# Linear attention, routed experts and a cosine layer in one program: values two slots behind the key maxima, a different pace of columns, routing in PSUM, four output buffers, rounding on DVE

## The chip, the cores and the metric

One Trainium2 chip, one of its cores. The metric is the device time of one execution in microseconds (us), as the median of several runs of the same program. All inputs start in device memory, and the result must lie there at the end. A core has TensorE (PE in the rows; PEld is its weight load), VectorE (DVE), ScalarE (ACT), GpSimd (POOL) and SyncE (SP, which here only issues transfers). Each engine takes its instructions strictly in the order in which they stand in its queue.

## The reference

Three layers follow one another. Attention without a score matrix (8 batches, 8 heads, 576 positions, 64 dimensions):

```
q_s = exp(q - max(q, -1));  q_s /= sum(q_s, -1) + 1e-9
k_s = exp(k - max(k, 2));   k_s /= sum(k_s, 2) + 1e-9
kv = einsum('bhsd,bhse->bhde', k_s, v)
x  = einsum('bhsd,bhde->bhse', q_s, kv)
```

Then 8 experts with two chosen per token (4608 tokens of width 512, inner width 1024), where the choice uses noisy logits:

```
noisy = x @ w_gate + log1p(exp(x @ w_noise)) * noise
top2 of noisy, softmax over the two -> weights
out += weight * (max(x @ w1[e], 0) @ w2[e])
```

And a last layer over all tokens with inner width 2048: `h = x @ w_in`, `y = (h * cos(h)) @ w_out`.

`w_in` and `w_out` come as 64-bit floats and are rounded to 32 bits on the chip.

## The kernel before

**Attention.** The keys of a batch are worked in two halves of four heads, so there are 16 half batches, and a loop gives each of them a slot `s`. `k_stage` takes one half batch: ACT copies half of the keys into PSUM (`kc`), DVE folds the four position groups and the 64 tail rows (`ktl`) into maxima `km` (L271 to L274), PE transposes `km` (`pkm`), DVE reduces it (`m`), PE spreads the maxima back over the partitions (`pkb`), ACT copies them (`mb`), POOL subtracts them from the keys, and ACT takes the exponential. `kv_stage` multiplies keys by values into `pkv` (L313), and after the second half of a batch DVE divides by the sums into `kvn` (L319 to L321). `kg_stage` transposes `kvn` on PE (`pkt`, L329) and multiplies it by the gate and noise weights (`pkg`), so that a token's logits come out with its x. The queries of 128 tokens form a column, and there are 36. `x_unit` transposes the queries of a column (`pqt`, ACT makes `qtt` of it), multiplies them by `kvn` into `px`, which has a single buffer, and DVE makes x (`xs`) and the logits (`lg`) of it (L392 to L398). The table `COLS` says how many columns each slot takes: 18 in the loop, 18 after it.

**Routing.** `routing` runs in three parts, after columns 18, 27 and 36. It is a chain of small DVE instructions on tiles of 144 or 72 elements per partition with a few ACT functions and matmuls between them, and ends in lists of tokens per expert. The first list lets the first three groups of tokens of expert 0 start while columns are still worked.

**Experts.** A group is up to 512 tokens of one expert. Per 128 inner elements a step does 12 matmuls into `ph` (`mm1`), ACT takes `hh` = relu, DVE takes the remainder `hl`, and two steps later 3 matmuls per 128 tokens go into `acc` (`mm2`). Numbers are kept as a pair of 32-bit values of reduced precision, high and low, hence three products. At a group's end `acc` is copied to a staging tile `ys`, by ACT for even blocks and by DVE for odd ones, and SP stores it to `y_d`. The next group's tokens are gathered by POOL into `xg`, moved by SP in four transfers per block (`xl<-xg`) and transposed by DVE. `w_load` brings expert weights through `wst` tiles; ACT makes the high part, POOL the low part. `convert` rounds the 64-bit weights in 64 pieces in the background of the first experts: SP loads `c`, ACT takes the magnitude (`ca`, L813), DVE does seven instructions, and SP stores the result from `cw`.

**Order.** The code is written in the order of the slots and steps, but a scheduler decides the final place of each instruction in its engine's queue, so a moved line can shift its neighbours too.

Of the kernel before, what the change touches and what calls it, by code (L numbers as in the profile page):

```python
# [10 lines left out]
F32 = mybir.dt.float32  # L11
# [16 lines left out]
def tile_attention_moe_moe2(  # L28
# [96 lines left out]
    def w_load(e):  # L125

        pend = []
        w1h, w1l, w2h, w2l = W[e % 2]

        def split():  # L130
            (kind, i, fh, _), st = pend.pop(0)
            if kind == 0:
                hi, lo = w1h[:, i, fh * 512:(fh + 1) * 512], w1l[:, i, fh * 512:(fh + 1) * 512]
            else:
                hi, lo = w2h[:, i, :], w2l[:, i, :]
            nc.scalar.activation(hi, st, AF.Copy)  # L136
# [40 lines left out]

    KB = 5
    QEB = 4
# [81 lines left out]
    def k_stage(j):  # L261
# [148 lines left out]
    def routing(t):  # L410
# [25 lines left out]
        nc.scalar.activation(ln, t1, AF.Ln)  # L436

        tiny = 2.0 ** -25
        d = tmp("rd")
# [5 lines left out]
        nc.vector.scalar_tensor_tensor(ln, z, 0.0, ln, op0=ALU.max, op1=ALU.add)  # L445
        yield
        tt(ln, ln, nzc, ALU.mult)
        l = tmp("ra")
        tt(l, ln, g, ALU.add)

# [3 lines left out]
        m2 = tmp("rm2", [P, n, 2, E])  # L454
        ta = tmp("rt1")
        for s in range(2):
# [26 lines left out]
        w2 = W2[:, cs, :]  # L483
        nc.vector.tensor_scalar(w2[:, :, 0], ex, 1.0, EPS, op0=ALU.add, op1=ALU.add)
        nc.vector.reciprocal(w2[:, :, 0], w2[:, :, 0])
        tt(w2[:, :, 1], ex, w2[:, :, 0], ALU.mult)
        yield
# [193 lines left out]

    HT = {}
    after = []

# [78 lines left out]
    def mm2(g, f):  # L763
# [42 lines left out]
    def convert():  # L806
        pend = []
        V = nc.vector

        def magnitude():  # L810
            t = pend[-1][1]
            ab = late[1].tile([P, CW], F32, name="ca", bufs=2)
            nc.scalar.activation(ab, t.bitcast(F32).rearrange("p (n w) -> p n w", w=2)[:, :, 1], AF.Abs)  # L813
            return ab

        def half1(ab):
# [12 lines left out]
        def half2(lo, bits, ab):  # L829
            dst = pend.pop(0)[2]  # L830
            w = late[1].tile([P, CW], F32, name="cw", bufs=2)
            V.tensor_single_scalar(ab, bits, -2 ** 23, op=ALU.bitwise_and)
            V.scalar_tensor_tensor(w, lo, 2.0 ** -52, ab.bitcast(F32), op0=ALU.mult, op1=ALU.mult)
            V.tensor_tensor(w, w, bits.bitcast(F32), op=ALU.add)
# [8 lines left out]
        for src, dst in jobs:  # L843
# [3 lines left out]
            if len(pend) == 2:  # L847
                yield
                z = half1(ab)
                ab = magnitude()  # L850
                yield
                half2(*z)
            else:
                ab = magnitude()
        yield
        half2(*half1(ab))

    C2 = 2.0 * math.pi - C1
    MAGIC = 1.5 * 2.0 ** 23
    magic = consts.tile([P, 1], F32, name="magic")  # L860
    nmagic = consts.tile([P, 1], F32, name="nmagic")
# [91 lines left out]
    presets(True)  # L953
    load_kv(1)
    load_kv(2)
    load_half(0, "q")
    load_kv(3)
    load_half(1, "q")
    load_kv(4)
    load_half(2, "q")  # L960
    COLS = {3: 1, 4: 2, 5: 2, 6: 2, 7: 1, 8: 2, 9: 1, 10: 2, 11: 1, 12: 1, 13: 1, 14: 1, 15: 1}
    QLOAD = {0: (3,), 2: (4, 5), 4: (6, 7), 11: (8,), 12: (9,), 13: (10,)}
    QST = {2: (0, 1), 4: (2, 3), 7: (4, 5), 9: (6, 7), 14: (8,), 15: (9,)}
    n = 0
    for s in range(2 * B + 1):
        if s < 2 * B:
            ks = k_stage(s)
            next(ks)
        if s >= 1:
            kv_stage(s - 1)  # L970
        if s == 0:
            load_small()
        if s >= 2 and s % 2 == 0:
            kg = kg_stage(s // 2 - 1)
            next(kg)
        if s in (4, 8):
            load_tail(s // 4 + 1, "k")
            load_tail(s // 4 + 1, "v")
        if s + KB < 2 * B:
            load_kv(s + KB)  # L980
        if s in (2, 6, 14):
            load_tail((2, 6, 14).index(s), "q")
        if s < 2 * B:
            finish(ks)
        if s >= 2 and s % 2 == 0:
            finish(kg)
        if s == 0:
            presets(False)
        next(cg, None)
# [4 lines left out]
        if s in (6, 11):  # L994
            q_tail((6, 11).index(s))
        for _ in range(COLS.get(s, 0)):
            x_unit(n)
            n += 1
    kp.release()
# [5 lines left out]
    mo = tc.alloc_tile_pool(name="mo", bufs=1, reuse_waits="tile")  # L1005
    for lst, name, k_, dt in ((HH, "hh", LAG + 1, F32R), (HL, "hl", LAG + 1, F32R), (YS, "ys", 2, F32)):
        lst += [mo.tile([P, 512], dt, name=f"{name}{j}") for j in range(k_)]
# [151 lines left out]
```

## Time and profile before

| | |
|---|---|
| median of 3 runs | 1955.85 us (1952.77 to 1956.34) |
| the profiled execution | 1950.03 us |
| its span, first to last instruction | 1947.9 us |
| busy: PE, DVE, ACT, POOL | 1822.6, 1135.4, 878.5, 450.6 us |
| mean granted TensorE clock | 0.958 |

The span is the profiled part of the execution; 2.1 us lie around it. The profiled execution was 5.8 us below the median of the runs. PE is busy for 94% of the span, so what can be gained lies where it waits, or where its clock is granted at 0.5 (1.2 GHz) and not at 1.0 (2.4 GHz). A busy sum over the whole span hides that the stages have different limits, so the stages are read apart.

### The profile page before, as it was taken

To read this page: it belongs to the slowest core of one execution; us is meant where nothing else is said; L and a number is where in the kernel's file an instruction comes from. 1 tells how busy PE (TensorE), PEld (TensorE's weight loads), DVE (VectorE), ACT (ScalarE), POOL (GpSimd) and SP (SyncE) were. 2 spreads that over 40 slices of the span, in tenths; PEclk is the share of its full clock that TensorE was granted. 3 is DMA by queue.
4 is the path that set the end of the run, shared out by engine and by line. 5 is a ranking of instruction groups with operands and counts; after the bars stand their busy time and mean duration, and the time that the engine had idled before them with its cause. 6 is when DMAs were issued, how large, how long until landed. Compare 5 with 4: busy or idle time off the path is not lost. (4 is left out here: it accounts for less than half of the span.)

```text
span 1947.9 us, 27149 instructions
## 1 busy us (share of the span) xinstructions
PE 1822.6 (94%) x9738; PEld 1535.1 (79%) x9738; DVE 1135.4 (58%) x2079; ACT 878.5 (45%) x1569; POOL 450.6 (23%) x405
## 2 busy tenths in 40 slices
PE   5777898989899999999999989999999999999998
PEld 4665787777777788989888878888888888888886
DVE  5768767776767743423333346665656565665654
ACT  4443333323224233232414256666666666666654
POOL 5445433504114023140405142110101010110000
PEclk7767899999999999999999999999999999999999
DMA  9942336645544434242425342202112030201000
GB/s 283 301 129 77 128 114 211 200 142 183 164 137 157 150 105 134 86 141 82 135 85 155 97 126 69 82 23 64 45 42 66 22 87 7 80 28 49 1 22 23
DMA packets 179776, 206.20 MB, mean 106 GB/s; under 512 B 34224, under 2 KB 121264, under 8 KB 179632
## 3 DMA queue, kind: packets, MB, share of 16 engines
q1 hardware_dynamic: 166896, 163.44, 27.1%
q0 software_dynamic: 12160, 39.86, 7.1%
q8 instruction: 82, 1.34, 0.3%
q10 hardware_dynamic: 576, 1.05, 0.1%
q14 instruction: 62, 0.51, 0.1%
HBM read 127.06 MB, written 49.43 MB: 91 GB/s over the span
## 5 line engine op out<-in xcount | busy, mean ns | idle before, releaser
L747 PE MATMUL ph<-xh,w1h 128*128 128x512 f32 (+2 forms) x1376 | 491.6, 357 | 7.4 <-DVE r L693 5.7
L748 PE MATMUL ph<-xl,w1h 128*128 128x512 f32 (+2 forms) x1376 | 491.3, 357 | 5.3 <-DVE xl L679 5.2
L749 PE MATMUL ph<-xh,w1l 128*128 128x512 f32 (+2 forms) x1376 | 491.2, 357 | 0.0
L771 PE MATMUL acc<-w2h,hh 128*128 128x512 f32 x1152 | 457.7, 397 | 23.6 <-ACT hh L753 8.7
L772 PE MATMUL acc<-w2l,hh 128*128 128x512 f32 x1152 | 453.5, 394 | 0.0
L773 PE MATMUL acc<-w2h,hl 128*128 128x512 f32 x1152 | 428.1, 395 | 13.6 <-DVE hl L754 13.0
L747 PEld LDWEIGHTS ph<-xh,w1h 128*128 128x128 f32 x1376 | 261.3, 190 | 47.5 <-DVE r L693 6.5
L748 PEld LDWEIGHTS ph<-xl,w1h 128*128 128x128 f32 x1376 | 261.5, 190 | 44.4 <-DVE xl L679 5.7
L749 PEld LDWEIGHTS ph<-xh,w1l 128*128 128x128 f32 x1376 | 261.8, 190 | 32.0
L771 PEld LDWEIGHTS acc<-w2h,hh 128*128 128x128 f32 x1152 | 218.6, 190 | 73.2 <-ACT hh L753 14.3
L773 PEld LDWEIGHTS acc<-w2h,hl 128*128 128x128 f32 x1152 | 216.7, 189 | 68.2 <-DVE hl L754 22.2
L754 DVE SCALAR_TENSOR_TENSOR hl<-ph,hh 128x256 fp32r<-128x256 f32 (+2 forms) x200 | 107.1, 539 | 259.5 <-ACT hh L753 259.2
L772 PEld LDWEIGHTS acc<-w2l,hh 128*128 128x128 f32 x1152 | 218.9, 190 | 40.0
L693 DVE SCALAR_TENSOR_TENSOR r<-r,ph 128x512 f32<-128x512 f32 x144 | 99.0, 687 | 142.6 <-ACT r L692 141.9
L616 POOL DMA_INDIRECT xg<-x_d,idx x80 | 78.1, 976 | 446.4 <-DVE xl L679 338.8
L753 ACT ACTIVATE hh<-ph 128x256 fp32r<-128x256 f32 (+2 forms) x200 | 93.0, 470 | 190.1 <-PE ph L749 185.2
L691 ACT ACTIVATE r<-r 128x512 f32<-128x512 f32 x144 | 90.7, 630 | 148.6 <-DVE r L690 148.6
L760 DVE TENSOR_TENSOR hl<-r,hh 128x512 fp32r<-128x512 f32 x144 | 99.3, 689 | 87.9 <-ACT hh L759 87.8
L616 POOL DMA_INDIRECT xg<-y_d,SL x36 | 34.8, 968 | 425.2 <-DVE xl L679 390.8
L137 POOL TENSOR_TENSOR w1l<-wst,w1h 128x512 fp32r<-128x512 f32 x80 | 103.1, 1312 | 123.0 <-ACT w1h L136 120.9
L689 DVE SCALAR_TENSOR_TENSOR r<-kk,ph 128x512 f32<-128x512 f32 x144 | 98.7, 685 | 48.9 <-ACT kk L688 48.6
L678 ACT ACTIVATE xh<-xg 128x512 fp32r<-128x512 f32 x106 | 66.6, 628 | 124.6 <-DVE xg L675 124.2
(184 smaller groups left out, 2208.5 us busy)
## 6 DMA issues: line engine op xcount, KB each, us to landing
wst<-in_moe_w_dram SPq DMA_DIRECT2D x128, 256.0 KB, 3.2
xl<-xg SPq DMA_DIRECT2D x396, 64.0 KB, 2.2
y_d<-ys SPq DMA_DIRECT2D x72, 256.0 KB, 2.3
kt<-in_k_dram SPq DMA_DIRECT2D x16, 512.0 KB, 6.7
vt<-in_v_dram SPq DMA_DIRECT2D x16, 512.0 KB, 7.2
qt<-in_q_dram SPq DMA_DIRECT2D x16, 512.0 KB, 7.2
x_d<-xs SPq DMA_DIRECT2D x32, 256.0 KB, 2.8
c<-in_moe_w_in_dram SPq DMA_DIRECT2D x32, 256.0 KB, 3.2
```

Of the source, the lines that this page charges most:

```text
L137: nc.gpsimd.tensor_tensor(lo, st, hi.bitcast(F32), op=ALU.subtract)
L616: return nc.gpsimd.indirect_dma_start(out=dst, out_offset=None, in_=src, in_offset=bass.IndirectOffsetOnAxis(ap=ix, axis=0))
L689: nc.vector.scalar_tensor_tensor(r, kk, -C1, ph, op0=ALU.mult, op1=ALU.add)
L693: nc.vector.scalar_tensor_tensor(r, r, 1.0, ph, op0=ALU.subtract, op1=ALU.mult, reverse0=True)
L747: nc.tensor.matmul(ph, w1h[:, kc, fs], g.xh[:, kc, :g.N], start=kc == 0, stop=False)
L748: nc.tensor.matmul(ph, w1h[:, kc, fs], g.xl[:, kc, :g.N], start=False, stop=False)
L749: nc.tensor.matmul(ph, w1l[:, kc, fs], g.xh[:, kc, :g.N], start=False, stop=kc == NK - 1)
L754: after.append(nc.vector.scalar_tensor_tensor(hl, ph, 0.0, hh.bitcast(F32), op0=ALU.max, op1=ALU.subtract))
L760: after.append(nc.vector.tensor_tensor(hl, r, hh.bitcast(F32), op=ALU.subtract))
L771: nc.tensor.matmul(g.acc[m], hh[:, ms], w2h[:, fr, :], start=f == 0, stop=False)
L772: nc.tensor.matmul(g.acc[m], hh[:, ms], w2l[:, fr, :], start=False, stop=False)
L773: nc.tensor.matmul(g.acc[m], hl[:, ms], w2h[:, fr, :], start=False, stop=f == g.nf - 1)
```

## The change

- The loop over slots gets two more slots. The product of keys and values of half batch j stands in slot j+2, the gate part of a batch another slot later, and the columns are spread anew by `COLS`, mostly one a slot. There are six key and value buffers and not five.
- The tail rows are folded into `kc`, which lies in PSUM, and no longer into `km`.
- In `routing` three tiles of the softplus and of the search for the two maxima lie in PSUM (`rs`), as does the reciprocal of the weights' sum; the magnitude and the addition of 1 go from DVE to ACT.
- There are four `ys` buffers in place of two, and the `y_d` stores of the blocks that ACT copies are issued by ACT. To make room, `wst` has three buffers in place of four.
- `convert` takes the magnitude on DVE with a bit mask, straight from the loaded piece; `ca` has three buffers and is also what is stored, and `cw` is gone.

```diff
@@ w_load
-            st = late[0].tile([P, 512], F32, name="wst", bufs=4)
+            st = late[0].tile([P, 512], F32, name="wst", bufs=3)
...
-            if len(pend) == 4:
+            if len(pend) == 3:
@@ k_stage
+        nc.vector.tensor_tensor(kc[rows, :, 1, :], ktl[rows, hs, :], kc[rows, :, 1, :], op=ALU.max)
         nc.vector.tensor_tensor(km, km, kc[:, :, 1, :], op=ALU.max)
-        nc.vector.tensor_tensor(km[rows], km[rows], ktl[rows, hs, :], op=ALU.max)
@@ routing
-        a = tmp("ra")
-        nc.vector.scalar_tensor_tensor(a, z, -1.0, z, op0=ALU.mult, op1=ALU.max)
+        rs = ps_at("rs", "sm", 1)[:, :3 * n * E].rearrange("p (x c e) -> p x c e", x=3, e=E)
+        d, l, ta = rs[:, 0], rs[:, 1], rs[:, 2]
         u = tmp("ru")
-        nc.scalar.activation(u, a, AF.Exp, scale=-1.0)
-        yield
+        nc.scalar.activation(l, z, AF.Abs)
+        nc.scalar.activation(u, l, AF.Exp, scale=-1.0)
         t1 = tmp("rt1")
-        nc.vector.tensor_single_scalar(t1, u, 1.0, op=ALU.add)
+        nc.scalar.activation(t1, u, AF.Identity, bias=one)
...
         tt(d, d, u, ALU.mult)
-        nc.vector.scalar_tensor_tensor(ln, ln, tiny, d, op0=ALU.max, op1=ALU.mult)
...
+        nc.vector.scalar_tensor_tensor(l, ln, tiny, d, op0=ALU.max, op1=ALU.mult)
@@ mm2
-                ys = YS[m % 2]
+                ys = YS[next(ysi) % 4]
...
-                nc.sync.dma_start(y_rows(g.e, g.b0 + m), ys)
+                eng = nc.scalar if m % 2 == 0 or g.i < NEARLY else nc.sync
+                eng.dma_start(y_rows(g.e, g.b0 + m), ys)
@@ convert
-            nc.scalar.activation(ab, t.bitcast(F32).rearrange("p (n w) -> p n w", w=2)[:, :, 1], AF.Abs)
...
+            ab = late[1].tile([P, CW], I32, name="ca", bufs=3)
...
-            V.tensor_scalar(ab, ab, EMIN, EMAX, op0=ALU.max, op1=ALU.min)
-            ab = ab.bitcast(I32)
+            V.tensor_single_scalar(ab, hi, 0x7fffffff, op=ALU.bitwise_and)
+            V.tensor_scalar(ab.bitcast(F32), ab.bitcast(F32), EMIN, EMAX, op0=ALU.max, op1=ALU.min)
...
-            w = late[1].tile([P, CW], F32, name="cw", bufs=2)
+            w = ab.bitcast(F32)
@@ the loop over slots
-    COLS = {3: 1, 4: 2, 5: 2, 6: 2, 7: 1, 8: 2, 9: 1, 10: 2, 11: 1, 12: 1, 13: 1, 14: 1, 15: 1}
+    COLS = {4: 1, 5: 1, 6: 2, 7: 1, 8: 1, 9: 1, 10: 1, 11: 1, 12: 1, 13: 1, 14: 1, 15: 1, 16: 2, 17: 2, 18: 1}
...
-        if s >= 1:
-            kv_stage(s - 1)
...
+        if 2 <= s < 2 * B + 2:
+            kv_stage(s - 2)
```

Where instructions stand shows what the scheduler made of it. On PE around the values product of half batch 7 (the operands `kt_309` before and `kt_334` after), before: `pkt_912` is the transpose of batch 3's `kvn`, and `pkm_928` that of the maxima of half batch 8.

```order
L313 MATMUL pkv_808<-v651_103,kt_309 64x65 x8
L313 MATMUL pkv_808<-vtl1_106,ktz1_93 64x65 x2
L313 MATMUL pkv_808<-v651_103,kt_309 64x65 x8
L313 MATMUL pkv_808<-vtl1_106,ktz1_93 64x65 x2
L384 MATMUL px_1075<-kvn2_96,qtt_991 128x81 x8
L368 MATMUL pqt_1183<-ident_75,qe_1060 128x128 x2
L368 MATMUL pqt_1183<-ident_75,qe_1064 128x128 x2
L329 MATMUL pkt_912<-ident_75,kvn3_97 64x128 x4
L280 MATMUL pkm_928<-ident_75,km_880 128x128 x2
```

The same place in the changed kernel; `pkb_827` belongs to half batch 8, `pkm_848` and `pkb_902` to half batch 9.

```order
L313 MATMUL pkv_806<-v651_103,kt_334 64x65 x3
L287 MATMUL pkb_827<-ident_75,m2_769 128x128 x2
L313 MATMUL pkv_806<-v651_103,kt_334 64x65 x5
L313 MATMUL pkv_806<-vtl1_106,ktz1_93 64x65 x2
L313 MATMUL pkv_806<-v651_103,kt_334 64x65 x4
L280 MATMUL pkm_848<-ident_75,km_840 128x128 x2
L313 MATMUL pkv_806<-v651_103,kt_334 64x65 x4
L313 MATMUL pkv_806<-vtl1_106,ktz1_93 64x65 x2
L287 MATMUL pkb_902<-ident_75,m2_851 128x128 x2
L384 MATMUL px_790<-kvn1_95,qtt_688 128x81 x8
L329 MATMUL pkt_931<-ident_75,kvn3_97 64x128 x4
```

The maxima of half batches 8 and 9 have moved ahead of the transpose that needs batch 3's quotient; before, those of half batch 8 stood behind it.

On DVE at the end of a group of expert 1, before (`c_5345` is a loaded piece of the 64-bit weights, `acc` a group's sum):

```order
L754 SCALAR_TENSOR_TENSOR hl_1676<-ph,hh_1673 128x384
L754 SCALAR_TENSOR_TENSOR hl_1677<-ph,hh_1674 128x384
L754 SCALAR_TENSOR_TENSOR hl_1678<-ph,hh_1675 128x384
L784 COPY ys_1680<-acc 128x512
L822 TENSOR_SCALAR ca<-ca 128x256
L824 TENSOR_SCALAR cb<-ca 128x256
```

The same place after (`L821` is the new mask, and `c_5321` and `c_5396` are the same two pieces as `c_5345` and `c_5419` before):

```order
L757 SCALAR_TENSOR_TENSOR hl_1679<-ph,hh_1676 128x384
L757 SCALAR_TENSOR_TENSOR hl_1680<-ph,hh_1677 128x384
L821 TENSOR_SCALAR ca<-c_5321 128x256
L787 COPY ys_1683<-acc 128x512
L822 TENSOR_SCALAR ca<-ca 128x256
L821 TENSOR_SCALAR ca<-c_5396 128x256
L823 TENSOR_SCALAR cb<-ca 128x256
L822 TENSOR_SCALAR ca<-ca 128x256
L787 COPY ys_1681<-acc 128x512
```

Each of the two copies of `acc` now stands behind a mask that reads a loaded piece.

## Rows read from the trace of the kernel before

**Rows 1.** Busy us by stretch; then PE clock, share of DMA engines, GB/s.

```profile
core 0: us, PE busy (x) PEld busy (x) DVE busy (x) ACT busy (x) POOL busy (x), PEclk, DMA share, GB/s
0.00:100.00 100.00, 64.88 (x714) 53.47 (x716) 67.26 (x151) 44.32 (x71) 52.73 (x65) 0.74 1.02 293
100.00:190.00 90.00, 65.26 (x806) 54.69 (x804) 72.46 (x184) 33.22 (x57) 40.26 (x29) 0.70 0.28 90
...
286.00:660.00 374.00, 336.30 (x1624) 280.94 (x1623) 274.05 (x557) 118.42 (x250) 109.43 (x91) 0.97 0.55 172
660.00:1948.00 1288.00, 1273.10 (x5993) 1074.57 (x5992) 656.31 (x1004) 650.82 (x1123) 214.08 (x191) 0.99 0.24 73
1144.00:1175.00 31.00, 25.18 (x96) 19.47 (x95) 17.92 (x21) 20.45 (x36) 22.25 (x19) 0.89 0.64 190
```

**Rows 2.** What PE waited for, 5 to 200 us: total, times, longest.

```profile
PE pkt L329 <- DVE kvn L321: 12.6, 5, 5.6
PE pkv L313 <- ACT kt L292: 8.1, 7, 3.1
```

**Rows 3.** What PE waited for, 100 to 190 us.

```profile
PE pkt L329 <- DVE kvn L321: 10.4, 4, 5.6
PE px L384 <- DVE lx L397: 6.2, 3, 3.4
...
PE pkv L313 <- ACT kt L292: 0.8, 1, 0.8
```

**Rows 4.** PE in order of time; idle before a row stands in brackets.

```profile
117.27 1.06 PE L329 MATMUL pkt<-ident,kvn 128*64 128x128 f32 x4 [5.56 <-DVE kvn L321]
```

**Rows 5.** Line L274: ns min/median/max, first and last start; whole span, then 100 to 190 us.

```profile
L274 DVE TENSOR_TENSOR km<-km,ktl x16: 416/422/4279, 7.4 to 154.7; 64x256 f32<-64x256 f32 x16
...
L274 DVE TENSOR_TENSOR km<-km,ktl x5: 416/422/423, 101.8 to 154.7; 64x256 f32<-64x256 f32 x5
```

**Rows 6.** DVE in order of time, first part of routing.

```profile
134.72 2.00 DVE L426 TENSOR_TENSOR rd<-rd,ru 128x144 f32<-128x144 f32 x1
...
136.82 1.82 DVE L444 SCALAR_TENSOR_TENSOR rln<-rln,rd 128x144 f32<-128x144 f32 x1
...
139.22 0.31 DVE L426 TENSOR_TENSOR rln<-rln,nz 128x144 f32<-128x144 f32 x1
```

**Rows 7.** What PE waited for, 290 to 700 us.

```profile
PE acc L773 <- DVE hl L754: 13.0, 14, 3.1
PE acc L771 <- ACT hh L753: 8.7, 7, 2.0
PE acc L771 <- DVE ys L784: 6.7, 2, 3.4
PE acc L771 <- ACT ys L782: 6.3, 2, 5.4
```

**Rows 8.** What ACT waited for, 290 to 700 us.

```profile
ACT ca L813 <- DMA c<-in_moe_w_out_dram: 62.7, 26, 7.7
ACT ca L813 <- DMA c<-in_moe_w_in_dram: 57.9, 23, 7.8
...
ACT w2h L136 <- DMA wst<-in_moe_w_dram: 29.3, 14, 4.8
ACT ys L782 <- DMA y_d<-ys: 22.6, 6, 8.0
```

**Rows 9.** What DVE waited for, 290 to 700 us.

```profile
DVE ca L822 <- ACT ca L813: 46.5, 36, 5.9
```

**Rows 10.** Instructions on the tile ca, as in rows 5.

```profile
L813 ACT ACTIVATE ca<-c x64: 416/432/454, 276.3 to 681.3; 128x256 f32<-128x256 f32 x64
L822 DVE TENSOR_SCALAR ca<-ca x64: 278/294/1394, 276.8 to 681.8; 128x256 f32<-128x256 f32 x64
```

**Rows 11.** SP, ACT and PE in order of time at a group's end.

```profile
392.65 5.55 SPq L643 DMA_DIRECT2D xl<-xg  x8
...
404.69 0.43 ACT L813 ACTIVATE ca<-c 128x256 f32<-128x256 f32 x1 [7.81 <-DMA c<-in_moe_w_in_dram]
...
408.75 0.80 PE L771 MATMUL acc<-w2h,hh 128*128 128x512 f32 x1 [5.35 <-ACT ys L782]
```

More of the change, by code (lines that the diff above doesn't have):

```diff
@@ L176, in load_tail @@
                               src[2 * t + b2, :, SM:, :].rearrange("h s d -> s h d"))
-    KB = 5
+    KB = 6
     QEB = 4
@@ L426, in tt @@
             eng.tensor_tensor(o, a, b, op=op)
-        a = tmp("ra")
-        nc.vector.scalar_tensor_tensor(a, z, -1.0, z, op0=ALU.mult, op1=ALU.max)
+        rs = ps_at("rs", "sm", 1)[:, :3 * n * E].rearrange("p (x c e) -> p x c e", x=3, e=E)
+        d, l, ta = rs[:, 0], rs[:, 1], rs[:, 2]
         u = tmp("ru")
-        nc.scalar.activation(u, a, AF.Exp, scale=-1.0)
-        yield
+        nc.scalar.activation(l, z, AF.Abs)
+        nc.scalar.activation(u, l, AF.Exp, scale=-1.0)
         t1 = tmp("rt1")
-        nc.vector.tensor_single_scalar(t1, u, 1.0, op=ALU.add)
+        nc.scalar.activation(t1, u, AF.Identity, bias=one)
         ln = tmp("rln")
         nc.scalar.activation(ln, t1, AF.Ln)
+        yield
         tiny = 2.0 ** -25
-        d = tmp("rd")
         nc.vector.tensor_scalar(d, t1, -1.0, tiny, op0=ALU.add, op1=ALU.max)
@@ L443, in routing @@
         tt(d, d, u, ALU.mult)
-        nc.vector.scalar_tensor_tensor(ln, ln, tiny, d, op0=ALU.max, op1=ALU.mult)
-        nc.vector.scalar_tensor_tensor(ln, z, 0.0, ln, op0=ALU.max, op1=ALU.add)
+        nc.vector.scalar_tensor_tensor(l, ln, tiny, d, op0=ALU.max, op1=ALU.mult)
         yield
-        tt(ln, ln, nzc, ALU.mult)
-        l = tmp("ra")
-        tt(l, ln, g, ALU.add)
+        nc.vector.scalar_tensor_tensor(l, z, 0.0, l, op0=ALU.max, op1=ALU.add)
+        tt(l, l, nzc, ALU.mult)
+        tt(l, l, g, ALU.add)
+        yield
         ie = ie100[:, None, :].to_broadcast(sh)
@@ L454, in routing @@
         m2 = tmp("rm2", [P, n, 2, E])
-        ta = tmp("rt1")
         for s in range(2):
@@ L483, in routing @@
         w2 = W2[:, cs, :]
-        nc.vector.tensor_scalar(w2[:, :, 0], ex, 1.0, EPS, op0=ALU.add, op1=ALU.add)
-        nc.vector.reciprocal(w2[:, :, 0], w2[:, :, 0])
-        tt(w2[:, :, 1], ex, w2[:, :, 0], ALU.mult)
+        wp = pr[:, 320:320 + n]
+        nc.vector.tensor_scalar(wp, ex, 1.0, EPS, op0=ALU.add, op1=ALU.add)
+        nc.vector.reciprocal(wp, wp)
+        tt(w2[:, :, 1], ex, wp, ALU.mult)
+        nc.scalar.activation(w2[:, :, 0], wp, AF.Copy)
         yield
@@ L682, in tile_attention_moe_moe2 @@
     HT = {}
+    ysi = itertools.count()
     after = []
@@ L808, in convert, with half1 @@
         V = nc.vector
-        def magnitude():
-            t = pend[-1][1]
-            ab = late[1].tile([P, CW], F32, name="ca", bufs=2)
-            nc.scalar.activation(ab, t.bitcast(F32).rearrange("p (n w) -> p n w", w=2)[:, :, 1], AF.Abs)
-            return ab
-        def half1(ab):
+        def half1():
             src, t, dst = pend[0]
@@ L830, in half2 @@
             dst = pend.pop(0)[2]
-            w = late[1].tile([P, CW], F32, name="cw", bufs=2)
+            w = ab.bitcast(F32)
             V.tensor_single_scalar(ab, bits, -2 ** 23, op=ALU.bitwise_and)
-            V.scalar_tensor_tensor(w, lo, 2.0 ** -52, ab.bitcast(F32), op0=ALU.mult, op1=ALU.mult)
+            V.scalar_tensor_tensor(w, lo, 2.0 ** -52, w, op0=ALU.mult, op1=ALU.mult)
             V.tensor_tensor(w, w, bits.bitcast(F32), op=ALU.add)
@@ L848, in convert @@
                 yield
-                z = half1(ab)
-                ab = magnitude()
+                z = half1()
                 yield
                 half2(*z)
-            else:
-                ab = magnitude()
         yield
-        half2(*half1(ab))
+        half2(*half1())
     C2 = 2.0 * math.pi - C1
     MAGIC = 1.5 * 2.0 ** 23
+    one = consts.tile([P, 1], F32, name="one")
+    nc.vector.memset(one, 1.0)
     magic = consts.tile([P, 1], F32, name="magic")
@@ L953, in tile_attention_moe_moe2 @@
     presets(True)
[L954 to L960, printed above, removed]
-    COLS = {3: 1, 4: 2, 5: 2, 6: 2, 7: 1, 8: 2, 9: 1, 10: 2, 11: 1, 12: 1, 13: 1, 14: 1, 15: 1}
-    QLOAD = {0: (3,), 2: (4, 5), 4: (6, 7), 11: (8,), 12: (9,), 13: (10,)}
-    QST = {2: (0, 1), 4: (2, 3), 7: (4, 5), 9: (6, 7), 14: (8,), 15: (9,)}
-    n = 0
[L965 to L968, printed above, removed]
-        if s >= 1:
-            kv_stage(s - 1)
+    for j in range(1, KB):
+        load_kv(j)
+        if j >= 2:
+            load_half(j - 2, "q")
@@ new lines, in tile_attention_moe_moe2 @@
+    COLS = {4: 1, 5: 1, 6: 2, 7: 1, 8: 1, 9: 1, 10: 1, 11: 1, 12: 1, 13: 1, 14: 1, 15: 1, 16: 2, 17: 2, 18: 1}
+    QLOAD = {3: (4, 5), 6: (6, 7), 12: (8,), 13: (9,), 14: (10,)}
+    QST = {3: (0, 1), 5: (2, 3), 10: (4, 5), 14: (6, 7), 16: (8,), 17: (9,)}
+    QTAIL = {9: 0, 16: 1}
+    n = 0
+    for s in range(2 * B + 3):
+        ks = k_stage(s) if s < 2 * B else iter(())
+        kg = kg_stage(s // 2 - 2) if s % 2 == 0 and s >= 4 else iter(())
+        todo = [n + i for i in range(COLS.get(s, 0))]
+        n += len(todo)
+        next(ks, None)
+        next(kg, None)
+        next(ks, None)
+        finish(kg)
+        if todo:
+            x_unit(todo.pop(0))
+        if 2 <= s < 2 * B + 2:
+            kv_stage(s - 2)
+        finish(ks)
+        if todo:
+            x_unit(todo.pop(0))
@@ L971, in tile_attention_moe_moe2 @@
         if s == 0:
             load_small()
[L973 to L987, printed above, removed]
-            presets(False)
@@ L989, in tile_attention_moe_moe2 @@
-        next(cg, None)
+            presets(False)
+        if s in (5, 9):
+            load_tail((s - 1) // 4 + 1, "k")
+            load_tail((s - 1) // 4 + 1, "v")
+        if 2 <= s and s + KB - 2 < 2 * B:
+            load_kv(s + KB - 2)
+        if s in (5, 10, 16):
+            load_tail((5, 10, 16).index(s), "q")
+        if s >= 4:
+            next(cg, None)
         for j in QST.get(s, ()):
@@ L993, in tile_attention_moe_moe2 @@
             load_half(j, "q")
[L994 to L998, printed above, removed]
+        if s in QTAIL:
+            q_tail(QTAIL[s])
     kp.release()
@@ L1005, in tile_attention_moe_moe2 @@
     mo = tc.alloc_tile_pool(name="mo", bufs=1, reuse_waits="tile")
-    for lst, name, k_, dt in ((HH, "hh", LAG + 1, F32R), (HL, "hl", LAG + 1, F32R), (YS, "ys", 2, F32)):
+    for lst, name, k_, dt in ((HH, "hh", LAG + 1, F32R), (HL, "hl", LAG + 1, F32R), (YS, "ys", 4, F32)):
         lst += [mo.tile([P, 512], dt, name=f"{name}{j}") for j in range(k_)]
```

## The prediction

> **What bounds the kernel now.** The busy times by stretch come first [rows 1], because PE is busy 94% of the span and only what is left can be gained. From 660 us on PE is busy 1273.1 of 1288.0 us at a clock of 0.99: nothing but PE's own work sets the pace there, and the change takes none of it away. Of the 14.9 us that PE stands there, 5.8 lie in the change to the last layer (31.0 less 25.2 between 1144 and 1175 us). Between 286 and 660 us PE is busy 336.3 of 374 us, so 37.7 are lost beside the rounding of the last layer's weights. The stretch from 100 to 190 us is the poorest: PE has 65.3 us of work in 90, at a granted clock of 0.70, so for most of it at 1.2 GHz. DVE has 72.5 us of work there, and the DMA engines 28%. The first 100 us look alike on PE (64.9 us of work), but the DMA engines are taken for the whole of them (share 1.02, 293 GB/s). What is lost to waits on engines in those first 100 us would for the most part be lost to loads if the engines were quicker.
>
> The second view is PE's waits. Up to 200 us the transpose of `kvn` waited 12.6 us for DVE and the values product 8.1 us for the exponential [rows 2]. In order of time one such wait is 5.56 us [rows 4], and what the reader is to see is what stands behind it on PE: `pkm`, the key maxima of the next half batch, which need nothing of `kvn`. So one late quotient delays the whole next key stage, which delays the next quotient. Of those 20.7 us, 11.2 lie after 100 us (10.4 and 0.8, [rows 3]).
>
> Between 290 and 700 us PE waited 15.0 us for ACT (`hh` 8.7, `ys` 6.3) and 19.7 us for DVE (`hl` 13.0, `ys` 6.7) [rows 7]. ACT's own waits tell why it was late [rows 8]: 62.7 and 57.9 us with the magnitude of a piece that had not landed, 22.6 us with a copy into a `ys` that was not stored yet, and 29.3 us with expert weights. An engine that waits holds everything behind it: at 404.69 us ACT had waited 7.81 us for a piece, while SP had spent 5.55 us on eight `xl<-xg` transfers alone, and at 408.75 us PE had stood 5.35 us for the `ys` copy behind it [rows 11].
>
> **The change part by part.** The sum is made against the profiled execution, 1950.0 us.
>
> *Values two slots later.* After it the rows on PE show `pkm` ahead of the transpose. I count the two waits as gone where loads do not stand behind them, after 100 us: 11.2 us. Nothing is counted for the 9.5 us before that, since the loads hide them; if the two extra buffers feed the loads better, they come on top. At most the cold clock goes too: 65.3 us of work at 0.70 would be 45.7 at 1.0, another 19.6 us. At the least nothing is gained, if PE meets the next wait (below). The two added slots contain no key stage, only products that the kernel did before as well. Term: -11 (-40 to 0).
>
> *Tail maxima in PSUM.* The instruction on two SBUF tiles took up to 4.28 us where 0.42 is the median; after 100 us the longest is 0.423 [rows 5]. All the gain is thus in the time that loads cover: counted at nothing. If that cover is gone, one such instruction is worth 3.9 us.
>
> *Routing in PSUM.* Two instructions took 2.00 and 1.82 us where the same shape takes 0.31 [rows 6]: 2.00 + 1.82 - 2 x 0.31 = 3.2 us of the chain to the first list, which opens the early groups. The two operations that move to ACT are costed at nothing: ACT has 33.2 us of work in 90 there [rows 1]. Term: -3 (-8 to 0; the upper gain is what five more such delays of 1 us would give).
>
> *Four output buffers, stores by ACT, and rounding on DVE* go together, since they free the same queue. The waits with the magnitude and with `ys` are 143.2 of ACT's listed 172.5 us, or 83%; of PE's 15.0 us for ACT that is 12.5. The Trainium skill has a rule that speaks against the stores: in "DMA: Bandwidth & Descriptors", section "Issuing engines are not separate DMA queues", issuing from several engines only saves the time to issue, since all transfers run on the same 16 engines. The row behind the 5.35 us stall is about SP's queue order, not about the engines; by the rule alone the 22.6 us would stay, 120.6 of 172.5 would go, and the term would be -10.5.
>
> The mask on DVE is new work: 64 instructions of the size of L822, at 0.294 us in the median and 1.394 at the worst [rows 10], so 19 to 89 us in a stretch where DVE has 274.1 of 374 us of work [rows 1]. I take 27 (0.42 each, nearer the median); DVE then has 301 us, 80%, and PE's two steps of slack hide it. ACT loses 64 x 0.432 = 28 us of work.
>
> I count no gain on PE's 19.7 us for DVE. The rows at a group's end show both copies of `acc` behind a mask, so DVE waits for the late pieces as ACT did. It waited 46.5 us for the magnitude already [rows 9]. Term: -12 (-30 to +48, the latter below).
>
> *Three weight buffers.* The split of a piece comes one load earlier. The expert steps hide it; the change to the last layer has no cover, and lost 5.8 us already. Term: +1 (0 to +4).
>
> Sum: -11 - 3 - 12 + 1 = -25, so 1925 us for an execution like the profiled one. That one ran 5.8 us below the median of its runs; the same distance puts the median at **1931 us**. Of no change a measurement tells about 0.2%, 4 us.
>
> **The rivals.**
>
> *The wait moves to DVE and becomes the bound (slower).* The place is the mask: behind it on DVE stand `hl`, the `ys` copies and the transposes, and PE waits for all three. ACT's waits for pieces were 120.6 us. If DVE takes all of them over, it has 301 us of work and 121 us of waiting in 374, 48 us too many: with the other terms the time is 1956 - 13 + 48 = 1991 us. It decides once DVE waits more than 374 - 301 = 73 us. For it speaks the order at the group's end; against it, that the code now has two steps between a piece's load and its use where the magnitude had one, and that DVE already bore 46.5 us of the same waits without being the bound. The Trainium skill, "SBUF — State Buffer", section "Who interferes with whom", says that a VectorE operation in a two-port mode and a GpSimd one exclude each other for a whole instruction. The 1.394 us is what that looks like here; if every mask met it, the 89 us would put DVE at 363 of 374 us and leave 11 us of room. Chance 0.10.
>
> *PE stands at the next wait in attention.* `px` has one buffer, and PE waited 6.2 us for DVE to empty it in the same 90 us [rows 3]; DVE has 80% of work there. Fewer columns lie in the key slots now, so more are left for the time of routing. Then the first term is nothing: 1931 + 11 = 1942 us. Chance 0.18.
>
> *Nothing between 286 and 660 us,* because what PE does not wait for on ACT it waits for on DVE's copies: 1931 + 12 = 1943 us. Chance 0.15.
>
> *The clock comes back.* With the gaps on PE gone the granted clock rises before 190 us: the first term is -11 - 9.5 - 19.6 = -40, and the time 1902 us. For it speaks that from 660 us on, where PE has hardly a gap, it is 0.99; against it, that the first 100 us are loads. Chance 0.17.
>
> *Both parts do nothing:* 1956 us, chance 0.06.
>
> **How the numbers follow.** The forecast itself has 0.34, the largest share, with its own range of 1918 to 1941. Reaching to the faster rival and past no change, the range is 1898 to 1957; it leaves out the slower rival (0.10) and an end of the clock's (about 0.06). Faster by over 0.2%, below 1952 us: the forecast, the clock, the third rival and most of the second, 0.34 + 0.17 + 0.15 + 0.14 = 0.80. Within 0.2%: 0.04 of the second, and most of the last, 0.09. Slower: the first rival and a little of the last, 0.11.
>
> **What would show each step.** Right: PE's wait for `kvn` below 3 us in attention, and the last product of keys and values before 180 us. ACT without a wait for a piece, and with under 5 us for `ys`; PE's waits for ACT after 290 us at 3 us or less. DVE waiting 40 to 70 us for pieces, with PE's waits for DVE near 20 us. PE's idle time between the early groups and 660 us near 25 us. The prediction is wrong if DVE waits over 73 us for pieces, if the granted clock before 190 us is above 0.85, or if PE's waits for `px` grow by what the others lose.

## The result, and the profile after

The changed kernel took 1935.7 us in the median (1932.1 to 1936.7, 4 runs) beside 1954.3 us of the kernel before in its 4 runs: a ratio of 0.9900, interval 0.9886 to 0.9915, so 1.0% faster. The forecast was 1931 us, with 1918 to 1941 as the range of the likeliest case, so the median lies in it, 5 us above the forecast. The two profiled executions are closer to each other, 1936.7 and 1950.0 us (spans 1934.6 and 1947.9): the one of before lay below its median. Traces can thus account for 13.3 us, not for 18.6.

PE's work is followed first. Busy times by stretch in the changed kernel, columns as in [rows 1]; 190 to 238 us is a stretch in which the last columns are worked:

```profile
0.00:100.00 100.00, 68.92 (x864) 56.05 (x864) 58.81 (x154) 55.52 (x89) 62.66 (x71) 0.80 1.04 283
100.00:190.00 90.00, 57.83 (x620) 48.02 (x620) 61.49 (x173) 30.82 (x58) 48.62 (x38) 0.68 0.43 137
...
190.00:238.00 48.00, 46.77 (x402) 40.95 (x405) 33.45 (x112) 13.74 (x32) 3.36 (x5) 0.93 0.25 81
...
286.00:660.00 374.00, 338.96 (x1620) 287.52 (x1619) 275.39 (x602) 99.62 (x193) 103.17 (x88) 0.96 0.54 167
```

The same 48 us in the kernel before:

```profile
190.00:238.00 48.00, 38.36 (x294) 33.40 (x293) 35.67 (x94) 17.86 (x36) 23.16 (x20) 0.82 0.46 146
```

What the reader is to see: between 100 and 190 us PE does less than before (57.8 us at a clock of 0.68, against 65.3 at 0.70), so the stretch on which the first term was built got no better by itself. The gain stands on both sides of it: 4.0 us more work in the first 100 us, at 0.80 and not 0.74, and 8.4 us more between 190 and 238 us, at 0.93 and not 0.82. (Second profiles of the two programs, below, show the same with 3.0 and 7.1 us.) Between 286 and 660 us PE has 339.0 us of work where it had 336.3.

PE's waits in the changed kernel, 100 to 190 us:

```profile
PE pqt L368 <- ACT qtt L370: 18.2, 8, 4.9
...
PE px L384 <- DVE lx L397: 4.7, 3, 2.4
```

The transpose of `kvn` is gone from this list, where it had 10.4 us [rows 3]; over 5 to 200 us it waits 1.2 us in all, once, where it had 12.6. In its place PE waits for ACT to empty `pqt` into `qtt`, a wait that the stretch did not have. The products of keys and values and the last column, in the rows of their lines (as in [rows 5]), first in the changed kernel and then in the one before:

```profile
L313 PE MATMUL pkv<-vtl,ktz x128: 222/240/370, 15.7 to 126.9; 128*64 128x65 f32 x128
...
L389 PE MATMUL px<-kvn,qtt x128: 227/230/281, 87.5 to 238.4; 64*64 64x81 f32 x128
```

```profile
L313 PE MATMUL pkv<-vtl,ktz x128: 222/315/367, 15.6 to 186.7; 128*64 128x65 f32 x128
...
L389 PE MATMUL px<-kvn,qtt x128: 227/232/395, 80.1 to 249.5; 64*64 64x81 f32 x128
```

The keys are done 60 us earlier, with most columns still to come, and the last column starts 11.1 us earlier. Of the 13.3 us only 2.2 are left for all that follows.

PE's, ACT's and DVE's waits between 290 and 700 us, which answer to [rows 7 to 9]:

```profile
PE acc L776 <- DVE hl L757: 19.7, 13, 3.5
PE acc L774 <- DVE ys L787: 9.7, 3, 3.7
PE acc L774 <- ACT hh L756: 4.7, 5, 1.7
PE ph L750 <- DVE hl L757: 1.4, 1, 1.4
```

```profile
ACT xh L680 <- DVE xg L677: 95.4, 34, 6.6
ACT hh L756 <- PE ph L752: 91.1, 30, 9.8
```

```profile
DVE ca L821 <- DMA c<-in_moe_w_out_dram: 33.9, 23, 5.4
...
DVE ca L821 <- DMA c<-in_moe_w_in_dram: 27.5, 16, 5.6
```

ACT does what was foreseen: it waits for no piece of the 64-bit weights and no store, most of all it waits for DVE and PE, and PE's waits for it fell from 15.0 to 4.7 us (3 or less was foreseen). But PE's waits for DVE rose from 19.7 to 30.8 us (19.7 + 9.7 + 1.4; 20.5 before, with two small rows that [rows 7] leave out). In sum PE waits as long as before: 35.5 us, from 34.7, or 36.4 from 37.4 with all the small rows. One such wait in order of time, first on SP, then DVE, then PE:

```profile
387.14 5.81 SPq L645 DMA_DIRECT2D xl<-xg  x8
393.06 2.48 SPq L645 DMA_DIRECT2D xh<-xg  x4
...
396.21 0.46 SPq L844 DMA_DIRECT2D c<-in_moe_w_in_dram  x1
...
400.17 0.29 DVE L821 TENSOR_SCALAR ca<-c 128x256 int32<-128x256 int32 x1 [5.58 <-DMA c<-in_moe_w_in_dram]
400.38 0.68 DVE L787 COPY ys<-acc 128x512 f32<-128x512 f32 x1
...
401.12 0.80 PE L774 MATMUL acc<-w2h,hh 128*128 128x512 f32 x1 [3.74 <-DVE ys L787]
```

This is the stall of [rows 11] again at the end of the same group: SP is 8.3 us with the next group's tokens, the load of the piece goes out behind them, the mask waits 5.58 us, and the copy of `acc` that PE needs stands behind the mask. It was 5.35 us by ACT and is 3.74 us by DVE.

### The profile page after: what moved, and what is told of

Its sections match the earlier page's. It is cut to its first block, busy times and chain, and to the rows that moved or that the text cites. A ratio compares the mean times of both kernels' runs of the same rounds, so it can differ in the third digit from the quotient of the medians.

```text
span 1934.6 us, 27003 instructions
## 1 busy us (share of the span) xinstructions
PE 1815.6 (94%) x9738; PEld 1531.3 (79%) x9738; DVE 1118.6 (58%) x2138; ACT 860.6 (44%) x1514; POOL 447.7 (23%) x405
## 5 line engine op out<-in xcount | busy, mean ns | idle before, releaser
L776 PE MATMUL acc<-w2h,hl 128*128 128x512 f32 x1152 | 427.7, 396 | 21.5 <-DVE hl L757 19.7
L774 PEld LDWEIGHTS acc<-w2h,hh 128*128 128x128 f32 x1152 | 218.2, 189 | 65.7 <-ACT hh L756 11.1
L618 POOL DMA_INDIRECT xg<-x_d,idx x80 | 76.8, 959 | 441.8 <-DVE xl L681 190.4
```

The source lines that it names most:

```text
L618: return nc.gpsimd.indirect_dma_start(out=dst, out_offset=None, in_=src, in_offset=bass.IndirectOffsetOnAxis(ap=ix, axis=0))
L774: nc.tensor.matmul(g.acc[m], hh[:, ms], w2h[:, fr, :], start=f == 0, stop=False)
L776: nc.tensor.matmul(g.acc[m], hl[:, ms], w2h[:, fr, :], start=False, stop=f == g.nf - 1)
```

## The experiments

All times are ratios to the kernel before, run beside them on the same chip. The profile of each kernel gives the start of the last column (row of `px`, as above) and of the experts' first product. "Weight buffers" is the number of `wst` tiles.

| kernel | weight buffers | first product | last column | from there to the end | ratio (interval) |
|---|---|---|---|---|---|
| before | 4 | 197.8 | 249.5 | 1698.4 | 1 |
| before_again | 4 | 198.0 | 250.9 | 1706.1 | |
| second_half | 3 | 202.1 | 248.8 | 1692.2 | 0.9940 (0.9920 to 0.9959) |
| loop_only | 4 | 195.6 | 237.9 | 1696.6 | 0.9948 (0.9926 to 0.9971) |
| first_half | 4 | 191.6 | 233.5 | 1695.4 | 0.9901 (0.9878 to 0.9923) |
| first_mask | 4 | 190.4 | 232.3 | 1697.5 | 0.9914 (0.9893 to 0.9936) |
| first_dve2 | 4 | 190.9 | 234.2 | 1696.9 | 0.9935 (0.9911 to 0.9959) |
| wst4_ys3 | 4 | 187.9 | 230.4 | 1697.9 | 0.9915 (0.9897 to 0.9933) |
| changed | 3 | 196.8 | 238.4 | 1696.2 | 0.9900 (0.9886 to 0.9915) |
| after_again | 3 | 197.3 | 238.9 | 1693.9 | 0.9918 (0.9897 to 0.9940) |
| col_step2 | 3 | 199.8 | 241.5 | 1693.6 | 0.9915 (0.9897 to 0.9932) |
| w_dve | 3 | 198.8 | 239.9 | 1697.0 | 0.9939 (0.9918 to 0.9959) |
| c3 | 3 | 195.3 | 237.1 | 1695.2 | 0.9948 (0.9930 to 0.9966) |
| no_round | 3 | 198.6 | 241.0 | 1662.7 | 0.9778 (0.9758 to 0.9799) |

(The fifth column is the span less the fourth.)

**How far one program differs from itself.** The changed kernel unaltered (after_again), the kernel before unaltered (before_again), and this edit:

```diff
@@ columns after the loop (col_step2)
-        wbg.step(4)
+        wbg.step(2)
```

> The changed kernel once more, unaltered, so that the kernels beside it can be set against it on one chip. Its median should lie within 3 us of 1935.7; the stretch up to the last column, which an almost identical program ended at 241.7 us where the changed one had 238.7, should again differ by about 3 us, which is then what a single profile can tell there.

> The kernel before once more, for a second profile: the profiled execution shown ran 4 us below the median of its runs. Where the last column ends (249.7 us) and how long the first layer of experts takes after it tell how far two executions of one program differ by stage; a difference of 3 us or less in each is expected, and any difference between kernels that is smaller is then no finding.

> The changed kernel, but two splits of expert weights behind a column in place of four; nothing else. Theory W: three buffers are enough for two splits, so ACT's wait for expert weights falls below 8 us between 100 and 200 us and PE's wait for qtt below 10, and the kernel is 3 to 9 us faster than the changed one. Rival R: within 3 us of 1936. If the weights then come too late for the first group of tokens, the first product of the experts comes later than 196.8 us and PE waits for w1h or w1l.

The edit of col_step2 moved nothing: the scheduler put every instruction where it stood, up to the numbers of buffers. Theory W was not tested by it, and it serves as a third run of the changed program. The three differ by 3.1 us at the last column, the two profiles of before by 1.4 there but by 7.7 after it (the execution of before_again took 1959.1 us). The ratios of one program go from 0.9900 to 0.9918. Single differences below that are no finding here; rows that repeat over several kernels are.

**The two halves.** second_half is the kernel before with the weight and output buffers, the stores by ACT and the mask; first_half is the changed kernel with those undone; loop_only also undoes the tail maxima and the routing.

```diff
@@ first_half, from the changed kernel (convert as before, with ACT's magnitude and cw)
-            st = late[0].tile([P, 512], F32, name="wst", bufs=3)
+            st = late[0].tile([P, 512], F32, name="wst", bufs=4)
...
-                ys = YS[next(ysi) % 4]
+                ys = YS[m % 2]
...
-                eng = nc.scalar if m % 2 == 0 or g.i < NEARLY else nc.sync
-                eng.dma_start(y_rows(g.e, g.b0 + m), ys)
+                nc.sync.dma_start(y_rows(g.e, g.b0 + m), ys)
```

> The attention loop, the tail maxima and the routing of the change alone; four weight buffers, two output buffers stored by SP and the magnitude on ACT as before. Theory W (in the changed kernel ACT's qtt copies stand behind splits of expert weights that wait for their pieces, 18.2 us between 100 and 200 us, because three weight buffers let one load less run ahead while a column asks for four splits; this ate a part of the attention gain): with four buffers ACT waits under 6 us for expert weights there, PE under 8 us for qtt where it waited 18.2, the last column lies before 234 us where the changed kernel had 238.7, and the time is 15 to 22 us below before, at or below the changed kernel. Rival R (DVE's routing chain sets the pace there, and the weights only fill its gaps): the last column stays within 3 us of 238.7, and the time is 10 to 14 us below before.

> Four output buffers, stores by ACT, three weight buffers and the mask on DVE alone, with the attention and the routing of before. The prediction's term: 11 us faster than before. Theory M (ACT's waits for late pieces have only moved to DVE, where they stand ahead of the copies and of hl): within 4 us of before, with PE's waits for ACT between 290 and 700 us down to about 5 us from 15.0 and its waits for DVE up by 8 to 12 us from 19.7.

> Only the new slot loop with six key and value buffers on the kernel before; tail maxima, routing, weights, output buffers and rounding as before. By the prediction's terms (-11 for the loop, -3 for the routing, nothing for the tail maxima) and the 16 us by which the last column came earlier with all three, the loop alone brings the last column 12 to 16 us earlier than 249.7 us, and 11 to 19 us of time. Rival R (the routing chain opens the early groups and sets the pace): the loop alone brings less than 8 us, the rest came from the routing in PSUM.

The loop alone takes 11.6 us off the last column and 10 us (6 to 14) off the time; with tail maxima and routing, which no run tells apart, it is 16.0 and 19 us (15 to 24). Both figures of loop_only lie just below what was expected of it, and rival R fell. In first_half theory W had the last column and the time right, but not its rows: ACT still waits 11.7 us for weights and PE 14.6 us for `qtt`. The loop brings two more slots, a sixth key and value buffer and a new table of columns, and these were not tried one by one either. The first half is as fast as the whole change. The second half alone is 0.6% faster than before: 10.8 us, which is the prediction's 11 and not within theory M's 4. Its rows are those of theory M all the same: PE's waits between 290 and 700 us are 32.4 us for DVE and 3.5 for ACT, no less in sum than before. On top of the first half the second adds nothing. From the last column on, the kernels with the mask need 1692 to 1698 us (mean 1695.4 without no_round), those with ACT's magnitude 1695 to 1706 (mean 1698.7, or 1696.8 without before_again): 1 to 3 us, which the scatter does not tell from nothing. Why second_half by itself gained 0.6% is open.

In loop_only the routing's tiles are all in SBUF; DVE and POOL in order of time:

```profile
142.59 1.82 DVE L440 TENSOR_SCALAR rd<-rt 128x144 f32<-128x144 f32 x1
...
145.54 2.04 DVE L426 TENSOR_TENSOR rd<-rd,ru 128x144 f32<-128x144 f32 x1
147.68 1.18 DVE L444 SCALAR_TENSOR_TENSOR rln<-rln,rd 128x144 f32<-128x144 f32 x1
...
142.43 1.89 POOL L347 TENSOR_TENSOR qe<-qt,qm 128x1024 f32<-128x1024 f32 x1
...
145.52 1.89 POOL L347 TENSOR_TENSOR qe<-qt,qm 128x1024 f32<-128x1024 f32 x1
```

The same steps in the changed kernel, with one operand in PSUM, and POOL busy all the while:

```profile
146.54 0.32 DVE L426 TENSOR_TENSOR rs<-rs,ru 128x144 f32<-128x144 f32 x1
...
146.97 0.31 DVE L445 SCALAR_TENSOR_TENSOR rs<-rln,rs 128x144 f32<-128x144 f32 x1
...
144.99 1.90 POOL L347 TENSOR_TENSOR qe<-qt,qm 128x1024 f32<-128x1024 f32 x1
146.85 3.72 POOL L137 TENSOR_TENSOR w2l<-wst,w2h 128x512 fp32r<-128x512 f32 x3
```

**The weight buffers.**

```diff
@@ wst4_ys3, from the changed kernel
-            st = late[0].tile([P, 512], F32, name="wst", bufs=3)
+            st = late[0].tile([P, 512], F32, name="wst", bufs=4)
...
-                ys = YS[next(ysi) % 4]
+                ys = YS[next(ysi) % 3]
```

> The changed kernel with four weight buffers again, and three output buffers to make room. Theory W: ACT waits under 6 us for expert weights between 100 and 200 us, where it was 18.2, the last column comes 4 us or more before 238.7 us, and the kernel is 4 to 10 us faster than the changed one, about 1928 us. Rival R: the wait is gone, but the last column stays within 3 us and the time within 3 us of 1936. A third output buffer too few would show as ACT waits for a ys store between 290 and 700 us, 22.6 us before the change and none after.

ACT's waits between 100 and 190 us, first in the changed kernel, then in wst4_ys3:

```profile
ACT w1h L136 <- DMA wst<-in_moe_w_dram: 9.6, 4, 4.8
ACT w2h L136 <- DMA wst<-in_moe_w_dram: 8.6, 4, 3.7
```

```profile
ACT w2h L136 <- DMA wst<-in_moe_w_dram: 9.2, 7, 3.8
...
ACT w1h L136 <- DMA wst<-in_moe_w_dram: 2.7, 3, 1.8
```

The last column came 8.0 us earlier. The table bears that out beyond one run: with routing in PSUM the four kernels with four buffers start it at 230.4 to 234.2 us (mean 232.6), the six with three at 237.1 to 241.5 (mean 239.5), 6.9 us apart, with no overlap. Theory W had the place right and not the rows: ACT still waits 11.9 us for pieces (theory: under 6), and PE's wait for `qtt` between 100 and 200 us is 15.3 us, no less than in after_again, which has 15.4 with three buffers. In time the gain is smaller and not clear: the profiled span is 1928.3 us, but the ratio 0.9915. The medians of the kernels with three buffers and routing in PSUM (no_round aside) lie 0.8 to 6.3 us above those with four that ran on the same chip.

The cost also belongs to the new loop. In second_half, with three buffers and the old loop, ACT waits 3.5 us for pieces between 100 and 190 us, and the last column is no later than before (the first product is, by 4.3 us):

```profile
L389 PE MATMUL px<-kvn,qtt x128: 227/232/394, 77.2 to 248.8; 64*64 64x81 f32 x128
```

In loop_only, with four buffers and the new loop, ACT waits 17.2 us for them.

```diff
@@ w_dve, from the changed kernel; first_dve2 does this and the next on first_half
-        nc.scalar.activation(w2[:, :, 0], wp, AF.Copy)
+        nc.vector.tensor_copy(w2[:, :, 0], wp)
@@ first_dve2 alone
-        nc.scalar.activation(t1, u, AF.Identity, bias=one)
+        nc.vector.tensor_single_scalar(t1, u, 1.0, op=ALU.add)
```

> The changed kernel with one instruction moved back: the copy of the reciprocal into the table of weights (L488) on DVE and not on ACT. Theory A (with three weight buffers ACT stands 4 to 5 us at a split whose piece has not landed, the copy stands behind it, and DVE's next step of routing waits 4.3 to 5.1 us for it, so that the first list and the early groups come as much later): that wait is gone, the first product of the experts comes 3 to 6 us before 196.8 us, the last column 3 to 6 us before 238.7, and the time is 2 to 6 us lower. Rival P (PE's waits for px and qtt in the columns set the end of the stage, not the list): the first product comes earlier, the last column within 2 us of where it was, the time unchanged.

> The first half alone (four weight buffers, two output buffers, rounding as before) with the addition of 1 and that copy back on DVE. In the first half DVE waited 6.8 us for the addition, which stood behind weight splits on ACT. Theory A: the first product of the experts comes 3 to 6 us before 191.6 us, the last column before 231 us where it was 233.7, and the time is 2 to 6 us below the first half, so the lowest of all so far, at about 0.987 of before. Rival P: no change beyond 2 us against the first half, 0.990.

DVE's waits between 100 and 190 us, first in the changed kernel, then in w_dve:

```profile
DVE dx L392 <- PE px L384: 6.3, 5, 1.6
DVE rw L426 <- ACT W L488: 4.5, 1, 4.5
```

```profile
DVE dx L392 <- PE px L384: 13.4, 8, 3.5
```

The 4.5 us behind ACT are gone, and DVE waits 7.1 us longer for `px`; the first product came at 198.8 us, not before 196.8. Theory A fell in both kernels (first_dve2 has the last column at 234.2 us, from 233.5, and 0.9935). Rival P had the last column right, but the first product did not come earlier. Several chains pass through ACT's weight splits (the table of weights, and `qtt`, `pqt`, `px`), and freeing one leaves the others. Which of them carries the 6.9 us is open.

**The rounding.** first_mask adds the mask to first_half and nothing else; c3 gives the pieces a third buffer.

```diff
@@ c3, from the changed kernel
-            t = late[1].tile([P, 2 * CW], I32, name="c64", bufs=2)
+            t = late[1].tile([P, 2 * CW], I32, name="c64", bufs=3)
...
-                ys = YS[next(ysi) % 4]
+                ys = YS[next(ysi) % 3]
@@ no_round, from the changed kernel
-            dst = pend.pop(0)[2]
...
-            nc.sync.dma_start(dst, w)
+            src, t, dst = pend.pop(0)
+            nc.sync.dma_start(dst, flat)
```

> The first half (loop, tail maxima, routing; four weight buffers, two output buffers stored by SP) with the mask on DVE added, and nothing else. Theory M (the waits for late pieces move from ACT to DVE and stay in front of what PE needs): within 4 us of the first half's 1931.0; ACT's waits for pieces (119.7 us between 290 and 700 us there) gone, DVE's waits for pieces at 50 to 65 us, PE's waits for ACT lower by 4 to 8 us and for DVE higher by as much (from 18.3). Its wait for a ys store (23.1 us on ACT) stays. The prediction's term: 8 to 11 us below the first half.

> The changed kernel with a third buffer for the loaded pieces of the 64-bit weights, and three output buffers to make room. Theory M (a load of a piece waits for its buffer, then stands behind the transfers of the next group's tokens on SP, and DVE waits with it): DVE's waits for pieces fall from 61.4 us to under 25 between 290 and 700 us, PE's waits for DVE there from 30.8 to under 20, and the kernel is 6 to 10 us faster than the changed one. Rival D (DVE's own work at 74% of that stretch is what PE waits for): DVE's waits for pieces fall, PE's waits for DVE stay above 25, and the time is within 3 us of the changed kernel.

> The changed kernel without the rounding's computation: the pieces are loaded and as many bytes are stored, but a constant tile is stored, and DVE does none of its eight instructions per piece (the last layer then works on a constant). Theory M, in its later form (PE's 36 us of idle time between 286 and 700 us come from DVE, by the rounding's work and its waits for pieces, whichever engine takes the magnitude): that idle time falls to 15 us or less, and the kernel is 18 to 25 us faster than the changed one. Rival O (the idle time belongs to the ends of the groups, their copies, gathers and transposes): it stays above 25 us, and the time falls by less than 10 us.

In first_mask ACT's 119.7 us of waits for pieces vanish, DVE waits 62.0 us for them, PE's waits go from 13.6 to 10.9 us for ACT and from 18.6 to 25.8 for DVE, and the ratio stays (0.9914 and 0.9901). PE's waits in it, 290 to 700 us:

```profile
PE acc L776 <- DVE hl L757: 17.1, 18, 3.4
PE acc L774 <- ACT hh L756: 10.7, 8, 4.9
PE acc L774 <- DVE ys L787: 6.9, 3, 2.6
```

That is theory M, but for two rows: PE's waits for ACT fell by 2.7 us and not by 4 to 8, and ACT's wait for a `ys` store did not stay at 23.1 us but rose to 49.6. wst4_ys3 has the stores by ACT and a third `ys` buffer on top of first_mask. ACT waits for no store there, PE's waits are 5.0 us for ACT and 26.0 for DVE, and the ratio is 0.9915: no gain in time is shown for the stores either.

DVE's waits in c3, 290 to 700 us:

```profile
DVE ca L821 <- DMA wo_d<-ca: 18.0, 10, 4.7
DVE ca L821 <- DMA c<-in_moe_w_out_dram: 13.7, 9, 3.4
DVE ca L821 <- DMA c<-in_moe_w_in_dram: 10.9, 7, 3.3
DVE ca L821 <- DMA wi_d<-ca: 9.9, 7, 3.7
```

The pieces come in time now (24.6 us of waits, from 61.4), and the mask waits 27.9 us for its own target instead, since `ca` is also what is stored. PE's waits for DVE stayed at 31.5 us. So c3 was no clean test of theory M or rival D: it took only 9 us of DVE's waits away, and gained nothing (its median is 4.9 us above that of after_again on the same chip).

no_round, without the computation: busy times from 286 to 660 us, and PE's only waits of more than 0.2 us, 290 to 700 us:

```profile
286.00:660.00 374.00, 360.52 (x1816) 312.06 (x1816) 119.02 (x179) 108.86 (x210) 107.81 (x93) 0.98 0.56 175
```

```profile
PE acc L774 <- ACT hh L756: 12.2, 5, 5.9
PE acc L774 <- ACT ys L785: 1.0, 1, 1.0
```

No wait for DVE is left, PE has 360.5 us of work in the 374 where it had 339.0, and all from the last column on is 30 to 35 us shorter than in the other kernels with the mask (1662.7 beside 1692.2 to 1697.9). By the ratios it is 24 to 27 us faster than the changed kernel, where theory M said 18 to 25. The loads, as many stores, and the copies and transposes at the ends of the groups are still there, so rival O fell. Of the 35.0 us in which PE stood idle in this stretch, 21.6 are thus lost to the rounding on DVE as a whole; 13.5 are not, nearly all of them waits for ACT.

What the run does not tell apart is DVE's work, its waits, and the waits that it causes on SP. In the changed kernel, 290 to 700 us, the loads of pieces stood on SP until DVE had done the last step that reads a piece and so frees its buffer:

```profile
SPq L844 <- DVE ca L832: 113.7, 33, 7.4
```

In no_round nothing waits for such a step, and in c3 this wait is 64.2 us.

## Why the prediction was right, and which terms were not

The time came out in the forecast's range. The first term had the right size, the mechanism of the largest one did not hold, and one small term hid a cost.

**The values two slots later (-11).** Right in size: loop_only has -11.6 us at the last column and -10 (6 to 14) in time. The reason was half right. PE's wait for `kvn` went as foreseen, and the last product of keys and values came at 126.9 us, well before 180. But I took the 11.2 us as gone from the stretch, and there 15.0 us of waits for `qtt` took their place in loop_only. By the rows the time came from the keys being done early: more work in the first 100 us, which I counted at nothing as hidden by loads, and columns and early groups with hardly a gap after 190 us. How much of it the two slots, the sixth buffer or the new table of columns brought is not shown. The rival of the next wait was thus right about what PE would meet, with `qtt` in place of `px`, and wrong that the gain would be lost.

**The clock.** Between 100 and 190 us it did not come back (0.68), as held most likely; above 0.85 before 190 us would have spoken against it. In the first 100 us it is 0.80, from 0.74. It rose from 0.82 to 0.93 between 190 and 238 us, where PE now has hardly a wait.

**Tail maxima and routing in PSUM (0 and -3).** loop_only to first_half gives -4.4 us at the last column, within the terms' bounds. The instruction on the tail rows, 4.28 us at the longest before [rows 5], is 0.440 at the longest after. Five routing steps on tiles in SBUF took 1.18 to 2.04 us there, where 0.3 us is the usual time. The two operations moved to ACT were costed at nothing. DVE waited 0.2 us for the addition in the changed kernel but 6.8 in first_half. A third one, which the prediction did not list, is the copy of the reciprocal into `W`, for which DVE waited 4.5 us in the changed kernel. Moving both back bought no time.

**Three weight buffers (+1).** The step that failed most plainly: "the expert steps hide it". I looked for the cost at the change to the last layer. It fell in the columns, where the weights of expert 0 are split: +6.9 us at the last column, though shown only with the new loop, and less in time.

**Buffers, stores and mask (-12).** Mis-sized: -1 to -3 us by the traces from the last column on, and nothing in time on top of the first half; that second_half alone gained 10.8 us stays unexplained. ACT's waits went nearly as computed, by 10.3 us on PE of the 12.5. The step that failed was "I count no gain on PE's 19.7 us for DVE", where a loss of 10 to 11 us had to be counted. PE's idle time between 286 and 660 us, to be near 25 us, is 35.0. The rival "nothing between 286 and 660 us", at 0.15, was the case here; its reason is nearly what the rows show: PE waits for DVE's copies (`ys`, 9.7 us from 6.7) and more for `hl` (19.7 from 13.0). The rival in which DVE becomes the bound did not come: its waits for pieces were 61.4 us, under the 73 named, and the mask was cheap:

```profile
L821 DVE TENSOR_SCALAR ca<-c x64: 252/294/516, 264.6 to 684.0; 128x256 int32<-128x256 int32 x64
```

64 of them are 19 us, not 27. The other seven steps take 181.8 us of the stretch (55 pieces fall into it) where they took 192.7 (57 pieces). So DVE has 275.4 us of work in 374 and not 301.

By the traces the sum is -11.6 - 4.4 + 6.9 - 2 = -11, beside 13.3 measured between the two profiles. Two errors, of 6 us in the weight buffers and 10 us here, separate the forecast's -25 from it.

**Luck.** With -11 for the sum, the prediction's own reckoning gives 1945 us and not 1931, so that the measured 1935.7 lies nearer to the forecast is in part luck. The medians moved by 18.6 us in the result, but by 16.3 and 15.1 when the changed program ran again (col_step2, after_again), beside 1952.8 and 1949.3 us of the kernel before and not 1954.3.

## What to carry to other kernels

A wait that is moved to another engine that executes in order is not removed: look at what stands behind it there, and at what the bound engine needs from that. Taking a stall away was worth its length only where other work was ready to fill the place. A buffer taken from a stream can cost far from the change, and together with another change more than alone, so look at all its uses.

## What the hardware showed that I had not expected

In these rows DVE instructions on SBUF tiles take as long as the POOL instructions beside them, one after another. In the changed kernel, on POOL, then DVE, then PE:

```profile
305.64 4.00 POOL L137 TENSOR_TENSOR w2l<-wst,w2h 128x512 fp32r<-128x512 f32 x3 [5.03 <-ACT w2h L136]
...
305.77 1.44 DVE L833 TENSOR_TENSOR ca<-ca,cb 128x256 f32<-128x256 f32 x1
307.24 1.27 DVE L823 TENSOR_SCALAR cb<-ca 128x256 int32<-128x256 int32 x1
308.55 1.37 DVE L824 SCALAR_TENSOR_TENSOR cb<-ca,cb 128x256 int32<-128x256 int32 x1
309.95 0.42 DVE L825 SCALAR_TENSOR_TENSOR cb<-c,cb 128x256 int32<-128x256 int32 x1
...
312.30 1.22 PE L776 MATMUL acc<-w2h,hl 128*128 128x512 f32 x2 [3.54 <-DVE hl L757]
```

Beside three weight splits of 1.3 us each, three rounding steps that take 0.3 to 0.4 us in the median took 4.1 us, and PE stood 3.54 us for the `hl` behind them: a stall before which DVE had waited no more than 1.43 us for a piece. The Trainium skill, "SBUF — State Buffer", section "Who interferes with whom", says that the two engines share a pair of ports which one instruction holds to its end, and that a DVE instruction with two inputs in SBUF contends with one of GpSimd that reads SBUF. The rows of the steps with two inputs agree (L833 and L824; the step between them, L823, reads a single tile and was held up too, 1.27 us, which that sentence does not cover). The rows of the routing agree from the other side: with one operand in PSUM, 0.32 us beside a busy POOL, where two in SBUF took 2.04.
